# Spreading dense products over the steps of attention, and two more products with the identity

## The chip, the cores and the metric

The kernel runs on one core of a Trainium2 chip. The metric is device time in microseconds (us) of one execution. The time before is 813.35 us, the median of three runs (808.65 to 816.64). PE is the matmul engine, DVE the vector engine, ACT the scalar engine, POOL the general one, SP the engine that issues most DMAs.

## The reference, cut to what matters

Everything is float32. Three blocks follow each other.

```python
def _attn_ref(q_l, k_l, v_l, q_g, k_g, v_g):        # 4 batches, 8 heads, 512 local + 32 global tokens, 64 deep
    out_g = np.matmul(sm(scale * q_g @ k_all.T), v_all)        # the global queries see all 544 keys
    s_ll  = np.where(np.abs(pos[:, None] - pos[None, :]) <= 32, scale * q_l @ k_l.T, -1e9)
    a_l   = sm(concat([scale * q_l @ k_g.T, s_ll]))            # the local ones a band and the 32 global keys
    return concat([out_g, a_l @ concat([v_g, v_l])])
def _moe_ref(x, w_in, w_out, alpha):                 # 2176 tokens, 512 -> 2048 -> 512
    h = x @ w_in
    return (np.maximum(h, 0) + alpha * np.minimum(h, 0)) @ w_out
def _moe2_ref(x, w_gate, w1, w2):                    # 8 experts, 512 -> 1024 -> 512
    ...                                              # greedy assignment of tokens with a capacity per expert
    out[mask] = np.maximum(x[mask] @ w1[e], 0) @ w2[e]
```

`sm` is a softmax over the last axis.

## The kernel before, in words

**Attention** is a loop of 34 steps (`attention`, L491 to L537). A unit is two heads of one batch, a pair is two units, and a pair takes four steps, j = 0 to 3, one for each 128 local queries. The loop is a software pipeline three deep. In step n it makes the scores of step n (PE L388, DVE L394, ACT L396), transposes the probabilities of step n - 1 (PE L410, ACT copy L412, after the DVE normalised them in L404), and multiplies those of step n - 2 with V (PE L421, ACT copy L423).

The work of the global queries of a pair comes in four pieces, one for each step (`pieces`): their scores (L437) at j = 1, nothing at j = 2, their transposes (L461, copied out by ACT and DVE in L462) at j = 3, and their product with V (`gpv`, L471) at j = 0 of the next pair, that is in steps 4, 8, 12, ... 32. L471 is 24 small float32 products of 32 columns.

**Dense work inside attention.** From step BEG = 12 on, PE also does part of the next block for the first 272 tokens (`dense`, L539 to L607). A dense piece is six products of 128x128 by 128x272 (L583, later L591). Two pieces make the first-layer result of one of eight feature blocks f; then comes an epilogue, one step later: ACT L546 (`neg`), DVE L561 (`g`), ACT and POOL L72/L73 (`ghi`, `glo`). The pieces of a step are issued after the scores and ahead of the global piece and of P V. `dense.at` counts them: 20 by the end of step 31, 22 in all.

**Products with the identity.** Before step 12 there is no dense work; there two products of the identity with itself (L521) go into the tile `o`, which P V overwrites afterwards. Nothing reads them.

**Weights.** `fill` puts the decoding of first-layer weights (`win`, eight parts, then `wout`) between the attention's instructions on DVE and ACT: about 2.7 DVE operations of 128x512 in each step. POOL makes the low halves (L73).

**Order.** In attention the orders of PE, DVE and ACT are as written, and a waiting instruction holds up all behind it on its engine. SP and POOL are ordered by the scheduler. After attention only PE keeps the written order; DVE and ACT are scheduled too. There `dense.rest` finishes the first 272 tokens: four results are copied out (ACT L604, `xd`) and stored. The next chunk's products (L200) start in the buffer from which the first of these copies reads. Behind that, PE works through the dense blocks to the end of the program.

Of the kernel before, what the change touches and what calls it, by code (L numbers as in the profile page):

```python
# [25 lines left out]
def tile_attention_moe_moe(ctx: ExitStack, tc: tile.TileContext, qkw, vw,  # L26
# [5 lines left out]
    E, _, FF = w1.shape  # L32
# [279 lines left out]
    with ExitStack() as at:  # L312
# [12 lines left out]
        BEG = SOLO + 4  # L325

        def bank(shape, name):
            pool, tag = pY, "y"
            if name == "s" and wide[0]:
                pool, tag = pS, "s"  # L330
            elif name == "s":
                pool, tag = ((pS, "s"), (pS, "s"), (pH, "h1"), (pH, "h1"))[turn[0] % 4]
                turn[0] += 1
            elif name in ("t", "gs0", "gt0"):
                pool, tag = pX, "x"
            return pool.tile(shape, F32, name=name, tag=tag)

        units = [(b, hp) for b in range(B) for hp in range(H // 2)]
        NU = len(units)
# [4 lines left out]
        STEPS = S // QS  # L344
# [26 lines left out]
        def scores(p, j):  # L371
            d = G[p]
            if j == 0:
                b, hp = units[2 * p]
                if hp == 0:
                    XB[b] = gx.tile([128, KD, ST], F32, name="xb", bufs=2)
                d["x"] = XB[b][:, hp:hp + 2]
            d["pr", j] = pp.tile([128, 4, KW], F32, name="pr")
            d["sm", j] = pp.tile([128, 4], F32, name="sm")
            d["mx", j] = pp.tile([128, 4], F32, name="mx")  # L380
            s = [bank([128, 2, KW], "s") for _ in range(2)]
            for ii in range(0, 4, 2):
                for e in range(2):
                    i = 4 * j + ii + e
                    for a in range(2):
                        u = 2 * p + a
                        for h, r in heads():
                            T.matmul(s[e][lane(2 * a + h, i), ii // 2], queries(u, i)[r], U[u]["k"][r, kpos(i):kpos(i) + KW],  # L388
                                     start=True, stop=True)
            for ii in range(4):  # L390
                i = 4 * j + ii
                m = mask[:, 0 if i == 0 else 2 if i == NQ - 1 else 1]
                sc = pp.tile([128, KW], F32, name="sc", bufs=4)
                V.tensor_tensor_reduce(out=sc, in0=s[ii % 2][:, ii // 2], in1=m, scale=-D ** -0.5, scalar=BIG,  # L394
                                       op0=OP.add, op1=OP.min, accum_out=d["mx", j][:, ii:ii + 1])
                A.activation(out=d["pr", j][:, ii], in_=sc, func=AF.Exp, bias=d["mx", j][:, ii:ii + 1], scale=-1.0,  # L396
                             accum_out=d["sm", j][:, ii:ii + 1])
            P.tensor_scalar(d["sm", j], d["sm", j], 1e-9, None, op0=OP.add)

        def norm(p, j):  # L400
            sm = G[p]["sm", j]
            V.reciprocal(sm, sm)
            pr = G[p]["pr", j]
            V.tensor_tensor(pr, pr, sm.unsqueeze(2).to_broadcast([128, 4, KW]), op=OP.mult)  # L404

        def ptrans(p, j):
            d = G[p]
            t = bank([128, 4, 128], "t")
            for ii in range(4):
                T.transpose(t[:, ii], d["pr", j][:, ii], ident)  # L410
            d["t", j] = tp.tile([128, 4, 128], F32, name="pt")
            A.copy(d["t", j], t)  # L412

        def pv(p, j, o=None):
            d = G[p]
            o = bank([128, 2, QS], "o") if o is None else o
            for ii in range(4):
                i = 4 * j + ii
                for a in range(2):
                    for h, c in heads():  # L420
                        T.matmul(o[c, a, WIN * ii:WIN * ii + WIN], U[2 * p + a]["v"][:, i, c],  # L421
                                 d["t", j][:, ii, lane(2 * a + h, i)], start=True, stop=True)
            at_out[0] = A.copy(d["x"][:, :, SG + QS * j:SG + QS * j + QS], o)  # L423
# [51 lines left out]
        def gout(p):  # L475
            for a in range(2):
                b, hp = units[2 * p + a]
                nc.sync.dma_start(out=xs[hp, :, b * ST:(b + 1) * ST], in_=G[p]["x"][:, a])
                U[2 * p + a] = None
            G[p] = None  # L480
            done[0] = 2 * p + 1
# [9 lines left out]
        def attention():  # L491
            todo = []

            def one():
                if todo:
                    x, f = todo.pop(0)
                    f()
                    yield x

            N = STEPS * NU // 2  # L500
            for n in range(N + 2):
                p, j = divmod(n, STEPS)
                if n < N and p and 2 * p + 2 < NU:
                    (load_qk, load_v)[j // 2](2 * p + 2 + j % 2)
                if n == SOLO - 1:
                    nc.sync.dma_start(out=ag, in_=gate)
                wide[0] = n >= SOLO
                dense.turn(n)
                if 1 <= n <= N:
                    norm(*divmod(n - 1, STEPS))  # L510
                if n < N:
                    scores(p, j)
                while later:
                    later.pop()()
                dense.close(n)
                fill("V", 2)
                o = None
                if n >= 2:
                    o = bank([128, 2, QS], "o")
                    for _ in range((0, 0, 2, 2)[j] if n < BEG else 0):  # L520
                        T.matmul(o[:, 0], ident, ident, start=True, stop=True)  # L521
                dense.products(n)
                for x in one():
                    pass
                fill("V", 2 if n >= SOLO and n % 3 == 0 else 1 if n < SOLO else 0)
                if n >= 2:
                    v, j2 = divmod(n - 2, STEPS)
                    pv(v, j2, o)
                    if j2 == STEPS - 1:
                        gout(v)  # L530
                if 1 <= n <= N:
                    ptrans(*divmod(n - 1, STEPS))
                if n > 2:
                    fill("A", 2)
                if n < N and j == 0:
                    todo += pieces(p)
                yield 0  # L537

        class dense:  # L539
# [24 lines left out]
            def products(n):  # L564
                if n < BEG:
                    return
                for _ in range((0, 1, 2, 1)[n % STEPS] if n < STEPS * NU // 2 else 2):
                    at, dense.at = dense.at, dense.at + 1
                    if at >= 2 * KH + KH - 2:
                        return  # L570
                    if at >= 2 * KH:
                        f, d = divmod(at - 2 * KH, 2)
                        if not f:
                            dense.ys.append(pH.tile([128, CH], F32, name="h1", tag="h1"))
                        for _ in dense.second(d, (2 * f, 2 * f + 1)):
                            pass
                        continue
                    f, half = divmod(at, 2)
                    if not half:
                        dense.ps = pH.tile([128, CH], F32, name="h1", tag="h1")  # L580
                    for k in range(2 * half, 2 * half + 2):
                        for i, (w, x) in enumerate(((0, 0), (0, 1), (1, 0))):
                            T.matmul(dense.ps, WI[0][:, w, k, f * 128:(f + 1) * 128], dense.x[x][:, k],  # L583
                                     start=k == 0 and i == 0, stop=k == KD - 1 and i == 2)
                    if half:
                        dense.over.append((f, dense.ps))
# [22 lines left out]
        def fill(kind, n):  # L609
            if not queue:  # L610
                return
            st, at = queue[0]
            while n and at == kind:
                try:
                    at = next(st)
                    n -= 1
                except StopIteration:
                    queue.pop(0)
                    if ahead_:
                        queue.append(ahead_.pop(0))  # L620
                        queue[-1][1] = next(queue[-1][0])
                    if not queue:
                        return
                    st, at = queue[0]
            queue[0][1] = at
# [48 lines left out]
    with tc.tile_pool(name="dc2", bufs=1, side="right") as dc, tc.tile_pool(name="pW", bufs=2, space=PSUM) as pW, \  # L674
# [4 lines left out]
        n = 0  # L679
# [20 lines left out]
    with ExitStack() as mo:  # L700
# [713 lines left out]
        for k in range(E):  # L1414
            n = 0.0
# [101 lines left out]
```

## Time and profile before

| | |
|---|---|
| median of three runs | 813.35 us (808.65 to 816.64) |
| the profiled execution's own time | 815.25 us |
| its span | 813.5 us |
| PE busy | 784.1 us (96%) |
| DVE busy | 451.3 us (55%) |
| ACT busy | 393.0 us (48%) |
| POOL busy | 371.2 us (46%) |
| mean granted clock of PE | 0.984 of full speed |

The profiled execution lies 1.9 us above the median. Attention ends near 156 us. "Issue" is idle time for which the profile names no releaser. A clock of 1.00 is 2.4 GHz, one of 0.50 is 1.2 GHz.

### The profile page before, as it was taken

The numbers are of one execution on the slowest core, as the hardware profiler recorded it, in microseconds if no ns is written. First come the engines' busy times: TensorE is split into PE (matmuls) and PEld (weight loads), VectorE is DVE, ScalarE is ACT, GpSimd is POOL, SyncE is SP. The second block draws the span as 40 slices with busy tenths as digits, with TensorE's granted clock in tenths as the row PEclk, the third lists the DMA queues.
The fourth block names the chain that finished last, engine by engine and source line by source line (L and its number), as shares of the span: only waits on it lengthen the run. The fifth ranks groups of instructions, "written<-read, shape, count | busy, mean of one in ns | idle before, by whom it ended". The sixth has DMA issues, their size and how long they took to land.

```text
span 813.5 us, 20853 instructions
## 1 busy us (share of the span) xinstructions
PE 784.1 (96%) x8282; PEld 730.3 (90%) x8282; DVE 451.3 (55%) x1547; ACT 393.0 (48%) x983; POOL 371.2 (46%) x348
## 2 busy tenths in 40 slices
PE   7889999999999999999999999999999999999996
PEld 4667777899999999999999999999989999989994
DVE  5888897355546622333343357776767778651210
ACT  5778786554455543333333434342465554454431
POOL 2233343043445443200000647663799989688611
PEclk9989898999999999999999999999999999999999
DMA  9978784343343122021312227333366766457510
GB/s 345 405 253 302 285 290 154 101 168 112 129 134 106 34 78 84 22 62 56 111 56 56 83 67 233 98 106 130 105 212 203 207 206 189 150 186 209 192 52 27
DMA packets 53850, 121.98 MB, mean 150 GB/s; under 512 B 4600, under 2 KB 26040, under 8 KB 51705
## 3 DMA queue, kind: packets, MB, share of 16 engines
q1 hardware_dynamic: 50825, 111.73, 41.8%
q0 software_dynamic: 2928, 8.92, 3.0%
q8 instruction: 65, 1.06, 0.5%
q14 instruction: 32, 0.26, 0.1%
HBM read 102.80 MB, written 17.83 MB: 148 GB/s over the span
## 4 chain that ended last, share of the span: by engine, by line
PE 80%; DVE 6%; issue 4%; ACT 4%; DMA 3%; POOL 2%; POOLq 0%; SPq 0%; DVEq 0%; ACTq 0%
PE h L200 22%; PE h L1273 10%; PE h L1117 10%; PE h L1137 9%; PE y L239 9%; PE o L421 3%; PE s L388 2%; PE t L410 2%; PE go L471 2%; PE h L1350 2%; PE lp L282 2%; ACT pr L396 1%; PE pc L953 1%; DMA raw<-in_moe_w_dram 1%; DMA raw<-in_moe_w_in_dram 1%
## 5 line engine op out<-in xcount | busy, mean ns | idle before, releaser
L73 POOL TENSOR_TENSOR m<-raw,m 128x1024 fp32r<-128x1024 f32 x64 | 152.1, 2400 | 16.4 <-ACT m L72 14.0
L200 PE MATMUL h<-xh,win 128*128 128x272 f32 x704 | 138.3, 291 | 1.5 <-ACT xd L245 1.5
L73 POOL TENSOR_TENSOR gr<-gb,gr 128x272 fp32r<-128x272 f32 x64 | 48.1, 775 | 149.6 <-ACT gr L72 149.2
L200 PEld LDWEIGHTS h<-xh,win 128*128 128x128 f32 x704 | 111.8, 188 | 3.9 <-issue 2.2
L1117 PE MATMUL h<-xsh,m 128*128 128x272 f32 x512 | 103.4, 294 | 0.2 <-issue 0.2
L200 PE MATMUL h<-xl,win 128*128 128x272 f32 x352 | 101.3, 288 | 0.0
L1273 PE MATMUL h<-gr,wout 128*128 128x272 f32 x672 | 95.1, 294 | 0.0
L1137 PE MATMUL h<-hh,m 128*128 128x272 f32 x448 | 91.4, 295 | 0.0
L1273 PEld LDWEIGHTS h<-gr,wout 128*128 128x128 f32 x672 | 87.0, 189 | 0.4 <-ACT gr L72 0.4
L239 PE MATMUL y<-ghi,wout 128*128 128x272 f32 x448 | 86.9, 290 | 0.0
L73 POOL TENSOR_TENSOR glo<-g,ghi 128x272 fp32r<-128x272 f32 x64 | 55.5, 872 | 67.9 <-ACT ghi L72 48.0
L72 ACT CAST m<-raw 128x1024 fp32r<-128x1024 f32 x64 | 65.9, 1049 | 41.6 <-DMA raw<-in_moe_w_dram 40.2
L1117 PEld LDWEIGHTS h<-xsh,m 128*128 128x128 f32 x512 | 81.7, 189 | 0.4 <-DVE home L968 0.4
L205 ACT ACTIVATE neg<-h 128x272 f32<-128x272 f32 x120 | 47.6, 397 | 70.0 <-PE h L200 69.4
L1117 PE MATMUL h<-xsl,m 128*128 128x272 f32 x256 | 74.0, 292 | 0.0
L206 DVE SCALAR_TENSOR_TENSOR g<-neg,al,h 128x272 f32<-128x272 f32 x56 | 27.4, 495 | 83.2 <-ACT neg L205 70.7
L1137 PEld LDWEIGHTS h<-hh,m 128*128 128x128 f32 x448 | 71.4, 188 | 0.9 <-issue 0.9
L239 PEld LDWEIGHTS y<-ghi,wout 128*128 128x128 f32 x448 | 70.9, 188 | 0.8 <-issue 0.8
L200 PEld LDWEIGHTS h<-xl,win 128*128 128x128 f32 x352 | 66.4, 189 | 0.0
L1137 PE MATMUL h<-hl,m 128*128 128x272 f32 x224 | 65.8, 294 | 0.0
L239 PE MATMUL y<-glo,wout 128*128 128x272 f32 x224 | 64.6, 288 | 1.1 <-POOL glo L73 1.1
L206 DVE SCALAR_TENSOR_TENSOR gb<-neg,al,h 128x272 f32<-128x272 f32 x64 | 31.3, 496 | 58.5 <-ACT neg L205 58.4
(286 smaller groups left out, 1650.4 us busy)
## 6 DMA issues: line engine op xcount, KB each, us to landing
raw<-in_moe_w_dram SPq DMA_DIRECT2D x64, 512.0 KB, 4.2
vv<-in_v_dram SPq DMA_DIRECT2D x16, 1024.0 KB
qk<-in_qk_dram SPq DMA_DIRECT2D x14, 720.0 KB, 9.8
raw<-in_moe_w_in_dram SPq DMA_DIRECT2D x16, 512.0 KB, 5.3
raw<-in_moe_w_out_dram SPq DMA_DIRECT2D x16, 512.0 KB, 3.6
xb<-xs SPq DMA_DIRECT2D x15, 544.0 KB, 4.3
xs<-xb SPq DMA_DIRECT2D x16, 272.0 KB, 5.4
xpart<-xd SPq DMA_DIRECT2D x32, 136.0 KB, 1.7
```

Source lines behind the costliest of these rows:

```text
L72: a = A.copy(hi, src)
L73: return a, (lo_eng or V).tensor_tensor(lo, src, hi.bitcast(F32), op=OP.subtract)
L200: T.matmul(ps, wi[:, w, k, fs], x[:, k], start=i == 0, stop=i == 3 * KD - 1)
L205: A.activation(out=neg, in_=ps, func=AF.Relu, scale=-1.0)
L206: epi[0] = V.scalar_tensor_tensor(g, neg, al1[:, hf * KH + f:hf * KH + f + 1], ps, op0=OP.mult, op1=OP.add)
L239: T.matmul(ps, wo[:, w, f, ds_], x[:, f], start=f == 0 and i == 0, stop=f == KH - 1 and i == 2)
L282: T.matmul(lp[r:r + 32], w, x, start=n < 4, stop=n >= LT - 4)
L388: T.matmul(s[e][lane(2 * a + h, i), ii // 2], queries(u, i)[r], U[u]["k"][r, kpos(i):kpos(i) + KW], start=True, stop=True)
L421: T.matmul(o[c, a, WIN * ii:WIN * ii + WIN], U[2 * p + a]["v"][:, i, c], d["t", j][:, ii, lane(2 * a + h, i)], start=True, stop=True)
L1117: T.matmul(ps, d["w1"][:, w, kk, f * 128:(f + 1) * 128], x[:, kk], start=kk == 0 and i == 0, stop=kk == KD - 1 and i == 2)
L1137: T.matmul(ps, d["w2"][:, w, f, ms], x[:, f], start=i == 0, stop=i == 3 * K3 - 1)
L1273: T.matmul(ps[j], wo[:, w, f, ds_], x, start=f == 0 and a == 0, stop=f == KH - 1 and a == 2)
```

## The change

Two lists of numbers are replaced. Products with the identity now also stand at j = 0, which adds two in step 4 and two in step 8, ahead of L471. The dense pieces of steps 12 to 31 go from 0, 1, 2, 1 in the four steps of a pair to 1, 1, 1, 1: one piece is taken from each j = 2 and put in the j = 0 two steps earlier. The number of pieces is unchanged, and by the end of step 31 there are 20 as before.

```diff
                 if n >= 2:
                     o = bank([128, 2, QS], "o")
-                    for _ in range((0, 0, 2, 2)[j] if n < BEG else 0):
+                    for _ in range((2, 0, 2, 2)[j] if n < BEG else 0):
                         T.matmul(o[:, 0], ident, ident, start=True, stop=True)
                 dense.products(n)
...
             def products(n):
                 if n < BEG:
                     return
-                for _ in range((0, 1, 2, 1)[n % STEPS] if n < STEPS * NU // 2 else 2):
+                for _ in range(1 if n < STEPS * NU // 2 else 2):
                     at, dense.at = dense.at, dense.at + 1
```

On PE, step 4 (L388 scores, L471 the global P V, L421 the local P V); the same stands in step 8:

```order
 L388 MATMUL s<-qk 32x128 x16
+L521 MATMUL o<-ident 128x128 x2
 L471 MATMUL go<-gt,vv 64x32 x24
 L421 MATMUL o<-pt,vv 64x32 x16
 L410 MATMUL t<-ident,pr 128x128 x4
```

The two products stand between the scores and the global P V.

On PE, step 12, the first with dense work (`h` is the result of feature block 0):

```order
 L388 MATMUL s<-qk 32x128 x16
+L583 MATMUL h_1122<-xh,win 128x272
+L583 MATMUL h_1122<-xl,win 128x272
+L583 MATMUL h_1122<-xh,win 128x272 x2
+L583 MATMUL h_1122<-xl,win 128x272
+L583 MATMUL h_1122<-xh,win 128x272
 L471 MATMUL go<-gt,vv 64x32 x24
 L421 MATMUL o<-pt,vv 64x32 x16
```

The piece that stood in step 13 is now ahead of the global P V; steps 16, 20, 24 and 28 get theirs in the same place, and one piece goes from each of steps 14, 18, 22, 26 and 30. With that, one of the two epilogues in each pair moves on ACT and DVE from j = 3 to j = 2.

On ACT, just after attention (`xd` are the copies of `dense.rest`, `mag` and `win` the decoding of the second half's weights). Before:

```order
L72 CAST xh<-xb 128x1088
L83 ACTIVATE mag<-raw 128x512
L604 COPY xd<-h_2692 128x272
L83 ACTIVATE mag<-raw 128x512
L604 COPY xd<-h_2781 128x272
L72 CAST win<-mag 128x512
L83 ACTIVATE mag<-raw 128x512
L205 ACTIVATE neg<-h_3099 128x272
```

With the change:

```order
L72 CAST xh<-xb 128x1088
L83 ACTIVATE mag<-raw 128x512 x2
L72 CAST win<-mag 128x512
L604 COPY xd<-h_2607 128x272
L604 COPY xd<-h_2703 128x272
L83 ACTIVATE mag<-raw 128x512
L205 ACTIVATE neg<-h_3103 128x272
```

The first copy now stands behind the second load's first decoding operation and behind the cast of the first part, where before it stood ahead of both.

## Rows read from the trace of the kernel before

**Rows 1.** The page: granted clock in 40 slices, then the chain by engine.

```profile
PEclk9989898999999999999999999999999999999999
...
PE 80%; DVE 6%; issue 4%; ACT 4%; DMA 3%; POOL 2%; POOLq 0%; SPq 0%; DVEq 0%; ACTq 0%
```

**Rows 2.** Stretches (from:to, length, busy by engine, clock, DMA): low clock.

```profile
40.08:43.49 3.41, 3.41 (x56) 2.27 (x54) 0.83 (x6) 1.11 (x3) 0.00 (x0) 0.50 0.41 161
57.15:63.97 6.82, 6.82 (x85) 5.25 (x85) 5.50 (x20) 4.81 (x19) 2.32 (x3) 0.50 0.91 362
94.69:101.52 6.83, 6.83 (x84) 5.15 (x82) 5.30 (x18) 5.09 (x20) 2.76 (x4) 0.50 0.69 250
132.24:139.07 6.83, 6.83 (x101) 5.86 (x102) 3.58 (x17) 2.83 (x12) 1.09 (x2) 0.50 0.30 86
```

**Rows 3.** PE by time (start, length, what, idle before): steps 8, 12, 20, 28.

```profile
37.56 1.94 PE L471 MATMUL go<-gt,vv 128*64 128x32 f32 x46 [0.90 <-issue]
...
54.91 1.59 PE L471 MATMUL go<-gt,vv 128*64 128x32 f32 x39 [0.62 <-ACT gt L462]
56.98 0.75 PE L471 MATMUL go<-gt,vv 128*64 128x32 f32 x9 [0.49 <-issue]
...
93.07 2.07 PE L471 MATMUL go<-gt,vv 128*64 128x32 f32 x48 [1.43 <-ACT gt L462]
...
131.08 0.41 PE L388 MATMUL s<-qk 64*32 64x128 f32 x5 [1.97 <-issue]
131.43 2.61 PE L471 MATMUL go<-gt,vv 128*64 128x32 f32 x48
```

**Rows 4.** PE by time: the global P V of step 16; waits of steps 6 and 10.

```profile
74.67 1.95 PE L471 MATMUL go<-gt,vv 128*64 128x32 f32 x48
...
31.17 0.54 PE L421 MATMUL o<-pt,vv 128*64 128x32 f32 x11 [1.66 <-issue]
...
48.03 1.12 PE L421 MATMUL o<-pt,vv 128*64 128x32 f32 x32 [0.90 <-ACT pt L412]
```

**Rows 5.** Stretches: steps 12 to 27; pairs at full clock; steps 28 to 31.

```profile
55.53:131.43 75.90, 71.38 (x1419) 57.40 (x1415) 67.39 (x251) 61.47 (x213) 30.73 (x40) 0.91 0.83 298
...
74.67:93.07 18.40, 16.73 (x360) 13.65 (x359) 17.40 (x64) 15.22 (x54) 7.79 (x11) 1.00 0.88 328
...
112.13:131.43 19.30, 16.94 (x361) 13.50 (x359) 17.91 (x66) 17.40 (x58) 10.28 (x12) 1.00 0.83 296
131.43:151.28 19.85, 19.85 (x340) 16.81 (x338) 13.14 (x52) 12.11 (x45) 4.03 (x8) 0.83 0.18 59
```

**Rows 6.** PE by time: one pair with the identity, one dense piece, what follows each.

```profile
32.82 0.71 PE L521 MATMUL o<-ident 128*128 128x128 f32 x4
33.37 0.82 PE L461 MATMUL gt<-ident,gpat 128*128 128x128 f32 x6
...
70.76 0.39 PE L583 MATMUL h<-xh,win 128*128 128x272 f32 x1
...
71.62 0.82 PE L461 MATMUL gt<-ident,gpat 128*128 128x128 f32 x6
```

**Rows 7.** ACT by time, step 19: a dense epilogue's cast, and the copy behind it.

```profile
92.14 0.40 ACT L72 CAST ghi<-g 128x272 fp32r<-128x272 f32 x1
92.45 0.57 ACT L462 COPY gt<-gt 128x512 f32<-128x512 f32 x1
```

**Rows 8.** POOL by time: low halves of tokens and weights used by early pieces.

```profile
51.25 1.84 POOL L73 TENSOR_TENSOR xl<-xb,xh 128x544 fp32r<-128x544 f32 x1 [0.31 <-ACT xh L72]
...
56.20 1.35 POOL L73 TENSOR_TENSOR win<-mag,win 128x512 fp32r<-128x512 f32 x1 [0.33 <-ACT win L72]
```

**Rows 9.** After attention: ACT by time, then PE's first product of L200.

```profile
162.25 0.39 ACT L604 COPY xd<-h 128x272 f32<-128x272 f32 x1
...
164.09 0.68 ACT L83 ACTIVATE mag<-raw 128x512 f32<-128x512 f32 x1 [1.46 <-DMA raw<-in_moe_w_in_dram]
...
164.94 0.63 ACT L72 CAST win<-mag 128x512 fp32r<-128x512 f32 x1
...
164.29 0.29 PE L200 MATMUL h<-xh,win 128*128 128x272 f32 x1
```

## The prediction

> **What bounds the kernel now.** I began with the page. PE is in 80% of the chain that ended last, and its granted clock is full everywhere except in the first fifth of the span, in four short dents [rows 1]. So a microsecond that PE loses in attention mostly moves the end, and the dents are the thing to look at. The stretches at low clock, cut out by the clock column, are one of 3.41 us and three of 6.8 us, 23.9 us in all at 1.2 GHz, and PE is busy through all of them [rows 2]. Then I looked at what PE did just before each dent. Each time it was the global P V (L471) of a step with j = 0, namely steps 8, 12, 20 and 28, and each time PE had stood idle beside it: 0.90 us, 0.62 and 0.49 us, 1.43 us, 1.97 us [rows 3]. Two of these five waits are for ACT's copy of the transposed global probabilities (L462); the other three are "issue", with no releaser. The global P V of step 16 came with no wait before it, and no dent followed [rows 4]; the same holds for steps 4, 24 and 32. On the other side, a wait of 1.66 us in step 6 and one of 0.90 us in step 10, in steps with the identity and without L471, were followed by no dent either [rows 4]. So in this trace neither the thin global P V alone nor a wait alone is followed by a fall; the two together are.
>
> Last, what limits attention if PE's clock stays up. In steps 12 to 27 DVE is busy 67.39 of 75.90 us. The pair whose stretch is wholly at full clock from 74.67 to 93.07 took 18.40 us with DVE busy 17.40; the one from 112.13 took 19.30 with DVE busy 17.91. In steps 28 to 31, which decode few weights, DVE has 13.14 of 19.85 us and ACT 12.11 [rows 5]. So DVE is close behind PE until step 27, and far behind it afterwards.
>
> **The change, part by part**, against the profiled execution's 815.25 us.
>
> *Two products with the identity in steps 4 and 8.* A pair of them takes from 32.82 to 33.37 [rows 6], 0.55 us. PE does not wait for anything around L471 of step 4, so there it is a plain cost, and I count it in step 8 too: +1.1. If the "issue" wait of step 8 covers its pair, half of that goes; nothing makes it negative by itself.
>
> *Clock in step 8.* The pair adds full-width products directly ahead of the thin ones. That is what steps 6 and 10 have, which waited and kept the clock. I take it that the 3.41 us come back to full speed: half of it, -1.7. Ends: 0 and -1.7.
>
> *One dense piece ahead of L471 in steps 12, 16, 20, 24 and 28.* A piece takes from 70.76 to 71.62, 0.86 us [rows 6]. It is the same piece that leaves j = 2, so its own time cancels. What is new is that it stands where PE waited for L462: 0.62 us in step 12 and 1.43 us in step 20 [rows 3]. Also, the epilogue that used to end in j = 3 now ends in j = 2, and with it the 0.40 us cast goes that stood directly ahead of L462 on ACT [rows 7]. So the waits for ACT shrink to little, and wide products come before the thin ones. I expect no fall of the clock in steps 12 and 20. In step 28 the 1.97 us "issue" wait may come back, but with a piece behind it.
>
> Does the piece have its operands? Piece 0 in step 12, at 54.3 us (54.91 less the wait of 0.62, [rows 3]), needs the low halves of the tokens, which POOL finished at 53.1. Piece 1 in step 13, a quarter of a pair's 18.40 us later, near 58.9 us, needs the fourth weight part, which POOL finished at 57.6 [rows 8]. Over a microsecond is left in each; a miss would cost that much once.
>
> *What the returned clock is worth in steps 12 to 27.* On PE alone, two dents of 6.82 and 6.83 us would give half, 6.8 us. But DVE's order and work stay the same. In the two pairs at full clock the time exceeded DVE's busy time by 1.00 and 1.39 us [rows 5], mean 1.2. Four pairs at DVE's busy time plus 1.2 make 67.39 + 4.8 = 72.2 us, against 75.90: **-3.7**. Ends: 0, if DVE grows slower beside a busier POOL, and -6.8 by PE. I take the value from the pairs at full clock since they are the nearest rows.
>
> *Steps 28 to 31.* Neither DVE nor ACT is near 19.85 us, so half of 6.83 us comes back: **-3.4**. Ends: 0, if the "issue" wait pulls the clock down again, and -3.4.
>
> *Just behind attention.* The order of ACT changes. The copy `xd` of the first dense result was done at 162.6. PE's first product of L200, in that copy's buffer, came at 164.29 without a wait [rows 9]. Now the copy stands behind the second `mag` (164.09, after a wait for its load) and behind the cast `win` (then from about 164.7, as it needs DVE's decoding). The cast and the copy end near 165.6, so PE waits **+1.3** us for the buffer. Ends: 0, if the load lands sooner or the delay is absorbed at PE's next wait, and 1.6 with the cast where it was. Behind the copy are queued the second copy, two stores on SP and the next epilogues; they have further buffers.
>
> SP's other differences are a weight load moved past two loads of V or past stores of `xs`; these land steps ahead of their use, and I cost them at nothing.
>
> Sum: +1.1 - 1.7 - 3.7 - 3.4 + 1.3 = -6.4, so 815.25 - 6.4 = **808.9 us, say 809**. The profiled execution stood 1.9 us above the median shown, so this is 4.4 us below that median, or 0.5%. A measurement of this kernel can tell about 1% (8.1 us) from no change, and the forecast lies within it.
>
> One rule of the Trainium skill speaks against a part of this. "TensorE: Matmul & The Clock Gate", in its part 4 on the transpose, which it describes as a product with the identity, says that such transposes do not count as PE being busy in the way other products do. If that held for the products with the identity added here, step 8 would keep its dent and the sum would be -4.7, or 810.5. The rows of steps 6 and 10 [rows 4] do not decide it, since no thin product stands there.
>
> **The rivals.**
>
> *Waits alone pull the clock down.* Then only the dents of steps 12 and 20 go, whose waits for ACT are filled. The "issue" waits in steps 8 and 28 are touched by nothing here, and their dents stay. +1.1 - 3.7 + 1.3 = -1.3: 814. For it: every dent has a wait beside it. Against it: steps 6 and 10. Chance 0.17. The same page, in its section on oscillation of the clock gate, puts the fall down to waits between bursts of products; the trace agrees only in part, as steps 6 and 10 waited 1.66 and 0.90 us and kept the clock.
>
> *DVE takes back steps 12 to 27.* The clock stays up, but PE then waits for DVE's `pr` and ACT's copies: +1.1 - 1.7 - 0 - 3.4 + 1.3 = -2.7: 812.5. For it: 17.4 to 17.9 us of DVE work in the pairs without a dent. Against it: these pairs still ended within 1.0 to 1.4 us of that. Chance 0.13.
>
> *DVE doesn't bind.* Its order has slack where PE used to be late. Then PE's own ceiling counts: +1.1 - 1.7 - 6.8 - 3.4 = -10.8: 804.5. Chance 0.12.
>
> *Slower: the dents move to j = 2.* Steps 14, 18, 22, 26 and 30 lose their second piece. If a fall now follows a wait in each, five stretches of 6.8 us instead of three cost 2 x 3.4 = +6.8, with the identity and the buffer +9.2: 824. With only as many dents as before it is +2.4: 817.7. It decides at the point where PE waits in j = 2, where it had no wait until now. Against it: nothing thin stands there besides the local P V, and steps 6 and 10 carry even less dense work. Chance 0.08 for both sizes together.
>
> **How the numbers follow.** The forecast has the remaining 0.50. From 803.5 to 815.5 the range takes in the forecast with the ends of its terms, both rivals at 812.5 and 814, and the one at 804.5. Outside are the slower rival (0.08) and the tails of the run-to-run spread, which was 8 us over three runs, about 0.1 more. Faster by over 1% means below 805.2: the rival at 804.5 and a little of the forecast, 0.15. Slower by over 1% means above 821.5: the larger size of the slower rival, 0.05. Within 1%: 0.80.
>
> **What would show it.** The clock in attention: 1.00 over steps 8 to 32, or at most one dent left. PE's row for L471 in steps 12 and 20 with no wait, or a small one, for L462. Steps 12 to 27 near 72 us, steps 28 to 31 near 16.5 us. A wait of about 1.3 us at the first L200, with ACT's `xd` as its releaser. If the dents remain and have an "issue" wait beside them, the first rival is right. If the clock is full and the pairs still take 18.5 to 19 us, DVE is the bound. If dents follow the steps with j = 2, the slower one is right. What would make the number wrong without touching the mechanism: other "issue" waits than before, since no row says where they come from, and a load that reaches ACT later just behind attention.

## The result, and the profile after

The changed kernel takes **814.13 us** (median of 20 runs, 807.89 to 821.02) against 808.83 us for the kernel before in the same session (20 runs, 803.42 to 818.10). The ratio is 1.0054, with a 95% interval of 1.0032 to 1.0076. So it is slower by half a per cent where a gain of half a per cent was forecast. The time itself lies inside the range given, 803.5 to 815.5 us, and on the 814 of the first rival, but only because the kernel before came out at 808.83 us and not at the 815.25 that the sums start from. The profiled execution took 819.53 us, with a span of 817.8 us and a mean granted clock of 0.985.

Two rows of the page first: the granted clock in 40 slices, and the chain that ended last, by engine.

```profile
PEclk9989997999999999999999999999999999999999
...
PE 71%; DVE 8%; DMA 5%; issue 5%; POOL 5%; ACT 4%; SPq 0%; POOLq 0%; ACTq 0%; DVEq 0%
```

PE's share of the chain is 71%, where it was 80%. The clock's row has two low digits in its first fifth, where it had three [rows 1]. By the clock column there are three low stretches up to 200 us, where there were four [rows 2]. Cut out as stretches (from:to, length, busy time of PE, PEld, DVE, ACT and POOL with instruction counts, clock, DMA share, GB/s), they are:

```profile
38.49:48.75 10.26, 10.26 (x136) 7.77 (x138) 5.19 (x21) 4.87 (x20) 1.56 (x3) 0.50 0.48 194
130.65:140.90 10.25, 10.25 (x129) 8.23 (x129) 5.30 (x22) 4.67 (x20) 1.90 (x4) 0.50 0.21 58
168.26:171.67 3.41, 3.41 (x18) 3.41 (x17) 0.50 (x1) 1.36 (x3) 0.77 (x1) 0.50 0.54 199
```

That is 23.92 us at 1.2 GHz, against 23.9 in the four dents of before [rows 2]. The dents of steps 12 and 20 are gone. Those of steps 8 and 28 are there, three times and one and a half times as long, and there is a new one 11 us behind the last P V. PE by time shows what stands beside them (start, length, what, idle time before):

```profile
38.14 0.29 PE L388 MATMUL s<-qk 64*32 64x128 f32 x1 [1.30 <-issue]
38.36 1.08 PE L521 MATMUL o<-ident 128*128 128x128 f32 x4
39.37 3.21 PE L471 MATMUL go<-gt,vv 128*64 128x32 f32 x48
...
58.76 1.95 PE L471 MATMUL go<-gt,vv 128*64 128x32 f32 x48
...
94.49 1.95 PE L471 MATMUL go<-gt,vv 128*64 128x32 f32 x48
...
129.79 0.44 PE L388 MATMUL s<-qk 64*32 64x128 f32 x12 [1.87 <-issue]
130.16 0.39 PE L591 MATMUL h<-ghi,wout 128*128 128x272 f32 x1
...
131.39 3.21 PE L471 MATMUL go<-gt,vv 128*64 128x32 f32 x48
```

The global P V of steps 12 and 20 has no wait for ACT any more, and the 1.95 us it takes there is what step 16 took at full clock [rows 4]; before it was 1.59 and 0.75 with a pause between them, and 2.07 [rows 3]. Beside that of steps 8 and 28 stands an "issue" wait, as before, 1.30 and 1.87 us long. The clock fell at 38.5 and 130.7 us, right behind these waits and before L471 began, at 39.37 and 131.39. So the thin products had no part in these two falls. The identity products had begun at 38.36 and the dense piece at 130.16, so they came too late to show whether they would have kept the clock up.

Six stretches that cover the whole span, cut at the starts of L471 in steps 4, 12 and 28, at the end of the last P V, and at the 5000th matmul from the end; first the kernel before, then after:

```profile
0.00:19.61 19.61, 13.62 (x258) 8.99 (x259) 10.10 (x50) 10.98 (x41) 4.85 (x25) 1.00 0.91 343
19.61:54.91 35.30, 30.65 (x693) 23.71 (x685) 28.73 (x115) 26.50 (x95) 8.91 (x15) 0.95 0.85 317
54.91:131.43 76.52, 72.00 (x1433) 58.02 (x1433) 68.01 (x251) 62.09 (x214) 31.35 (x40) 0.91 0.83 298
131.43:156.73 25.30, 24.57 (x457) 21.04 (x455) 13.37 (x53) 13.06 (x47) 4.03 (x8) 0.87 0.14 47
156.73:215.84 59.11, 57.61 (x454) 57.23 (x455) 29.96 (x47) 27.52 (x62) 22.92 (x23) 1.00 0.49 160
215.84:813.48 597.64, 585.70 (x5002) 561.26 (x5000) 301.17 (x1033) 252.85 (x527) 299.11 (x239) 1.00 0.38 118
```

```profile
0.00:21.22 21.22, 14.91 (x262) 10.01 (x262) 10.90 (x55) 11.96 (x43) 4.84 (x25) 1.00 0.92 350
21.22:58.76 37.54, 35.13 (x696) 27.23 (x695) 28.37 (x110) 25.78 (x95) 9.34 (x15) 0.86 0.78 286
58.76:131.39 72.63, 67.44 (x1433) 54.14 (x1432) 68.81 (x258) 62.07 (x215) 30.52 (x40) 1.00 0.86 311
131.39:157.12 25.73, 25.00 (x450) 21.04 (x449) 12.33 (x47) 12.20 (x45) 3.29 (x7) 0.81 0.14 46
157.12:219.07 61.95, 59.40 (x454) 58.80 (x455) 30.08 (x47) 28.01 (x62) 22.91 (x23) 0.97 0.47 151
219.07:817.76 598.69, 586.04 (x5002) 561.21 (x5000) 301.22 (x1033) 252.58 (x527) 299.05 (x239) 1.00 0.38 118
```

The differences are +1.61, +2.24, -3.89, +0.43, +2.84 and +1.05 us, together +4.28. Only the third came near its forecast. The fifth, called the **tail** below, is the stretch behind attention. ACT and then PE there:

```profile
161.85 0.67 ACT L83 ACTIVATE mag<-raw 128x512 f32<-128x512 f32 x1 [3.31 <-DMA raw<-in_moe_w_in_dram]
165.52 0.66 ACT L83 ACTIVATE mag<-raw 128x512 f32<-128x512 f32 x1 [3.00 <-DMA raw<-in_moe_w_in_dram]
166.08 0.60 ACT L72 CAST win<-mag 128x512 fp32r<-128x512 f32 x1
166.59 0.67 ACT L604 COPY xd<-h 128x272 f32<-128x272 f32 x2
```

```profile
167.03 0.39 PE L200 MATMUL h<-xh,win 128*128 128x272 f32 x1 [2.18 <-ACT xd L604]
```

The second `mag` waits 3.00 us for its load, where it waited 1.46 [rows 9], and `xd` is queued behind it. So PE waits 2.18 us for `xd`, and 1.2 us later the low stretch from 168.26 begins. The wait of 1.50 us that PE had at 193.14 us in the kernel before (for ACT's `xd` of L245) is gone in turn.

### The profile page after: what moved, and what is told of

Read it like the earlier page. It is cut to its first block, busy times and chain, and to the rows that moved or that the text cites. A ratio compares the mean times of both kernels' runs of the same rounds, so it can differ in the third digit from the quotient of the medians.

```text
span 817.8 us, 20869 instructions
## 1 busy us (share of the span) xinstructions
PE 787.9 (96%) x8290; PEld 732.4 (90%) x8290; DVE 451.7 (55%) x1547; ACT 392.6 (48%) x983; POOL 369.9 (45%) x348
## 4 chain that ended last, share of the span: by engine, by line
PE 71%; DVE 8%; DMA 5%; issue 5%; POOL 5%; ACT 4%; SPq 0%; POOLq 0%; ACTq 0%; DVEq 0%
PE h L200 21%; PE h L1273 10%; PE y L239 9%; PE h L1117 8%; PE h L1137 7%; POOL m L73 3%; PE o L421 2%; DMA raw<-in_moe_w_dram 2%; DMA raw<-in_moe_w_in_dram 2%; PE h L1350 2%; PE lp L282 1%; PE s L388 1%; DVE pr L404 1%; PE go L471 1%; PE t L410 1%
## 5 line engine op out<-in xcount | busy, mean ns | idle before, releaser
L200 PE MATMUL h<-xh,win 128*128 128x272 f32 x704 | 139.8, 293 | 2.5 <-ACT xd L604 2.2
L200 PEld LDWEIGHTS h<-xh,win 128*128 128x128 f32 x704 | 113.0, 190 | 5.1 <-ACT xd L604 2.4
L200 PE MATMUL h<-xl,win 128*128 128x272 f32 x352 | 102.0, 290 | 0.0
L73 POOL TENSOR_TENSOR glo<-g,ghi 128x272 fp32r<-128x272 f32 x64 | 55.1, 866 | 69.7 <-ACT ghi L72 57.6
L200 PEld LDWEIGHTS h<-xl,win 128*128 128x128 f32 x352 | 67.1, 191 | 0.0
```

The source lines that it names most:

```text
L73: return a, (lo_eng or V).tensor_tensor(lo, src, hi.bitcast(F32), op=OP.subtract)
L200: T.matmul(ps, wi[:, w, k, fs], x[:, k], start=i == 0, stop=i == 3 * KD - 1)
```

## The experiments

Each was timed in five rounds beside the kernel before, with 12 runs of its own; one per cent of the time is 8.1 us, and a ratio's interval is about 0.3% either way. "Clock" is the mean granted clock over a kernel's runs; over the 163 runs of the kernel before it is 0.989. A low stretch is one at 1.2 GHz, as a dent is.

**The copy or the work in attention?** In e1, and in all labels with xd_first, the first `xd` is put ahead of the decode on ACT. e2 and e3 have the pieces alone, e4 the identity products alone:

```diff
     def win_part(pool, hf, i):
-        whole(win_steps(pool, hf, i))
+        ...                                    # part 0 up to its Abs, part 1 up to its load
+        with tc.issue_after(dense.freed.ins):  # freed: the copy of the first xd
+            whole(st)                          # the rest of the two
```

e1_after_xd_first: 

> The change, with ACT's copy of the first dense result behind attention put back ahead of the weight decoding, as it stood before. Theory A (the copy's new place is the loss): the 2.2 us wait at the first L200 and the dent behind it go, about 3.2 us, so that the time is at 1.000 to 1.002 of before, with only the 1.1 us of the four identity products left. Rival B (the new work in attention is the loss: the identity, the pieces, the dents of steps 8 and 28): 1.004 to 1.006, as the change itself.

Measured: 813.67 us, ratio 1.0049 (1.0013 to 1.0084), clock 0.991.

e2_pieces_xd_first: 

> One piece in each step, no added identity, the copy ahead of the decoding. Theory A: 0.997 to 1.001, the 1.1 us of the identity less than the first kernel of this set. Rival B with the pieces at fault: 1.004 or more; with the identity at fault: 1.000.

Measured: 812.68 us, 1.0032 (1.0001 to 1.0062), clock 0.991.

e3_pieces_only: 

> One piece in each step, no added identity; here the copy stands behind the decoding as in the change. Theory A: 3 to 4 us (0.4 to 0.5%) slower than the same kernel with the copy first, so 1.002 to 1.005 of before, and a wait of about 2 us at the first L200. Rival B: the same time as that kernel, whatever the wait.

Measured: 813.94 us, 1.0069 (1.0029 to 1.0108), clock 0.990.

e4_identity_xd_first: 

> The identity products in steps 4 and 8 alone, dense pieces as before, the copy ahead of the decoding. Theory A: 1.1 us slower than before, 1.001. Rival B with the identity at fault: 1.003 or more. If the identity keeps the clock up in step 8: 0.998.

Measured: 816.0 us, 1.0073 (1.0041 to 1.0105), clock 0.987.

The place of one copy is not the loss by itself: e1 stays at 1.005. Each half of the change alone also comes out slower here, at 1.003 to 1.007, and the intervals don't tell it from the whole. In e1 the wait at 167 us is gone, but another has taken its place further on. ACT of e1, then PE (line numbers are 7 higher):

```profile
190.75 0.77 ACT L252 COPY xd<-y 128x272 f32<-128x272 f32 x2 [2.20 <-DMA xpart<-xd]
```

```profile
191.18 0.39 PE L207 MATMUL h<-xh,win 128*128 128x272 f32 x1 [2.75 <-ACT xd L252]
```

The third of four `xd` copies waits for the store of the first, since `xd` has two buffers, and PE waits for the copy. In the kernel before the same PE wait was 1.50 us. So in e1 ACT is late again at the end of this stretch, and part of what its beginning gave back is lost there: the tail takes 60.51 us, 61.95 in the changed kernel and 59.11 before.

**The tail's order put back, and taken to the kernel before.** e5, e6 and e7 (change, pieces alone, identity alone) order ACT as Abs (`mag`), `xd`, Abs, `xd`, cast (`win`), and put the first store ahead of the fourth weight load. e8 leaves attention as before and gives the tail the order of the changed kernel; to get it, the first two weight parts are decoded earlier.

e5_after_tail_as_before: 

> The changed kernel with the order just behind attention put back nearly as it was before the change: ACT goes Abs, xd, Abs, xd, win cast (in the first try, e1, the second xd copy still stood behind the win cast and a second Abs), and SP issues the first store of xd ahead of the fourth raw load. In the traces so far the third xd copy waits for the first store (1.13 us before the change, 1.91 in e1, counted on ACT), the Relus behind it on ACT run 1.05 us later against the end of the last P V, and so does the decode that ends in the 2.75 us wait of the first product of the next block for ACT's xd (1.5 before). Theory T (the tail behind attention is worth 2 to 3 of the 5 us): 810.5 to 811.5, ratio 1.002 to 1.0035, what is left being the identity products (1.1 us) and some 1 us of the moved pieces. Rival R (the new work inside attention is the whole loss, whatever stands behind it): ratio 1.005 to 1.006 as in e1.

Measured: 814.28 us, 1.0034 (1.0003 to 1.0065), clock 0.990.

e6_pieces_tail_as_before: 

> Only the pieces (one in each step), no identity products at j = 0, with the order behind attention as before the change. Theory T: ratio 1.000 to 1.002 (in the stretches without low clock the moved pieces cost 0.15 to 0.4 us in each group of four steps, some 1 us in all). Rival R: 1.003 to 1.005, as e2 and e3.

Measured: 814.09 us, 1.0031 (0.9994 to 1.0068), clock 0.990.

e7_identity_tail_as_before: 

> Only the two identity products in each of steps 4 and 8, with the order behind attention as before the change. Theory T: 1.001 to 1.002 (their own 1.1 us), if the mean granted clock is that of the kernel before. Rival R: 1.004 to 1.007 as e4. If the granted clock is again lower than before (0.987 against 0.990 in e4), then the identity products themselves bring low stretches, some 0.75 us per us of lost clock, whatever the tail.

Measured: 814.25 us, 1.0013 (0.9974 to 1.0053), clock 0.989.

e8_before_tail_as_after: 

> The kernel before, attention untouched, with the order just behind attention as the changed kernel has it: ACT goes Abs, Abs, win cast, xd, xd, and SP issues the fourth raw load ahead of the first store of xd. Theory T: 1.0025 to 1.004 (2 to 3 us later; a wait of some 2 us of PE for ACT's xd and, behind it, a possible low stretch). Rival R: 0.999 to 1.001.

Measured: 812.69 us, 1.0017 (0.998 to 1.0053), clock 0.988.

Inconclusive as ratios, and the traces say why. The tail of e5 is no shorter than that of the changed kernel, and that of e8 is shorter than before (e5, then e8):

```profile
151.08:212.78 61.70, 59.17 (x455) 58.77 (x455) 30.09 (x47) 27.90 (x62) 22.93 (x23) 0.97 0.46 149
```

```profile
153.18:211.71 58.53, 57.43 (x455) 57.21 (x455) 28.40 (x47) 27.88 (x63) 22.53 (x23) 1.00 0.50 162
```

Neither kernel had the tail that its name promises. e5 still had PE wait 2.53 us for the third `xd`; e8's earlier decode took that wait away.

**The place in the instruction stream.** In the ten traces so far every "issue" wait of PE above 0.25 us in attention had come at the same count of instructions in PE's stream (matmuls, weight loads and semaphore instructions together): 194 or 195 over a multiple of 256. In the kernels with moved pieces the waits of 1.7 us or more had low stretches beside them. PE of e3:

```profile
95.58 0.53 PE L421 MATMUL o<-pt,vv 128*64 128x32 f32 x5 [2.01 <-issue]
...
118.34 0.83 PE L388 MATMUL s<-qk 64*32 64x128 f32 x21 [2.55 <-issue]
```

Small products ahead of the first scores move all that follows in the stream:

```diff
             N = STEPS * NU // 2
+            o = bank([128, 2, QS], "o")
+            for _ in range(16):                 # 32, 48, 32 in e10, e11, e12
+                T.matmul(o[:1, 0, :1], ident[:, :1], ident[:, :1], start=True, stop=True)
             for n in range(N + 2):
```

e9_after_shift64: 

> The changed kernel with 16 products of one column put ahead of the first scores, where TensorE waits for the first load anyway; nothing else changes but the place of every later TensorE instruction in the instruction stream, some 64 further. In all ten traces so far TensorE's waits that the profile calls issue fall at the same count of TensorE instructions (matmuls and weight loads), 194 or 195 over a multiple of 256. In the kernels with the moved pieces two of them are long (2.0 to 2.3 us some 4.9 us behind the sixth global P V's predecessor, in step 21, and 1.7 to 2.6 us in step 25) and each has a low stretch behind it. Theory F (the loss is where these waits fall): they come at the same counts, so some 2.5 us earlier in the program; lengths change, and the ratio is no longer 1.005: anywhere from 0.998 to 1.006, and at least one of the three shifts (64, 128, 192) gives 1.002 or less. Rival W (the moved work itself costs the time): 1.004 to 1.007 for all three.

Measured: 811.29 us, 1.0021 (0.9988 to 1.0054), clock 0.994.

e10_after_shift128: 

> As e9 with 32 such products, a shift of some 128 instructions, half of a block: the long waits come some 5 us earlier in the program than in the changed kernel. Theory F: another ratio than 1.005, between 0.998 and 1.006, and with e9 and e11 at least one at 1.002 or less. Rival W: 1.004 to 1.007.

Measured: 810.69 us, 1.0017 (0.9983 to 1.005), clock 0.994.

e11_after_shift192: 

> As e9 with 48 such products, a shift of some 192 instructions: the waits come some 7.5 us earlier, or 2.5 us later counted from the block before. Theory F: another ratio than 1.005, and with e9 and e10 at least one at 1.002 or less. Rival W: 1.004 to 1.007.

Measured: 814.12 us, 1.005 (1.0019 to 1.0082), clock 0.992.

e12_before_shift128: 

> The kernel before with 32 products of one column ahead of the first scores: its attention is unchanged, only its instruction stream is shifted by half a block (the order on ACT behind attention comes out as in the changed kernel, which e8 priced at 0.5 us). Theory F: the waits of 0.3 to 2.0 us in its steps 7, 9, 13 and 28 move to other places, so that the time moves too, by as much as 4 us (0.996 to 1.006), and the places of its low stretches with it. Rival W: 0.999 to 1.002, low stretches beside the global P V of steps 12, 20 and 28 as before.

Measured: 815.52 us, 1.0064 (1.0036 to 1.0092), clock 0.985.

The waits moved as the count says. In e9 one stands inside the global P V of step 16, where the unshifted kernel's trace has none:

```profile
76.91 1.30 PE L471 MATMUL go<-gt,vv 128*64 128x32 f32 x29 [0.74 <-issue]
```

Two of three shifts came below 1.0025, with the highest clocks so far, which favours theory F, though the intervals of e9 and e10 reach to that of the unshifted kernel. No shifted trace has the dent of step 28, but among the kernels with the moved pieces only the changed kernel's own trace has it; e1, e2, e3, e5 and e6 have none there either. e12 does not separate the two theories and lies just outside both ranges: its tail came out in the changed kernel's order and took 63.12 us, 4.0 more than before.

**Both, and the buffer.** e13 is the change with e8's tail, e14 adds the shift by 128, e15 is the pieces alone with such a shift, and e16 is the kernel before with three buffers for `xd`:

```diff
-                    xd = gx.tile([128, CH], F32, name="xd", bufs=2)
+                    xd = gx.tile([128, CH], F32, name="xd", bufs=3)
```

e13_after_tail_ahead: 

> The changed kernel with the stretch behind attention as in e8: the first two parts of the second half's weights are decoded some 4 steps of the generator earlier (at 6 and 7 in place of 10 and 20), so that ACT's decode chain no longer ends later than TensorE's block at 190 us. From the last P V to the 5000th matmul from the end e8 took 58.5 us and the kernel before 59.1, the changed kernel 62.0 and e5, e6 and e7, whose order was put back in part only, 61.3 to 61.7. Theory T (this stretch is some 2.5 of the 5 us that the change costs at equal clock): 58 to 59.5 us there, ratio 1.000 to 1.003. Rival N (the stretch evens out, as e5 seemed to say): ratio 1.004 to 1.006.

Measured: 813.97 us, 1.0041 (1.0011 to 1.007), clock 0.990. The tail is 59.84 us; for the time it is a miss for theory T.

e14_shift128_tail_ahead: 

> The changed kernel with the instruction stream shifted by some 128 instructions (e10) and the stretch behind attention as in e13. Theories F and T together: e10's 1.0017 less some 2.5 us, 0.997 to 1.0005, and a mean granted clock of 0.994 or more. If only F holds: 1.001 to 1.003. If the two gains exclude each other because a wait gained ahead is lost at the rendezvous with ACT at 190 us: 1.001 to 1.002, with that wait longer by as much.

Measured: 812.83 us, 1.0026 (0.9994 to 1.0058), clock 0.993. A miss for both together; "only F" fits.

e15_pieces_shift_tail: 

> Only the pieces, no identity products at j = 0, with 36 products of one column ahead of the first scores, so that the blocks of instructions fall on the same products from step 12 on as in e10; the stretch behind attention as the scheduler gives it. Theory F: e10's 1.0017 less the identity products' 1.1 us (0.0014), so 0.999 to 1.002, low stretches as rare as in e10 (mean clock 0.992 or more). Rival W: 1.003 to 1.005, as e3 and e6.

Measured: 814.68 us, 1.0041 (1.0008 to 1.0073), clock 0.991. A miss for theory F.

e16_before_three_xd: 

> The kernel before with a third buffer for xd, so that the third copy doesn't wait for the first store (1.13 us on ACT at 170 us, 2.00 us at 192.7 us, the latter with the first product of the next block waiting 1.50 us behind it). Theory T: that wait of TensorE falls from 1.5 us to 0.5 us or less, ratio 0.997 to 0.9995. Rival N: no change, 0.999 to 1.001.

Measured: 809.91 us, 1.0005 (0.9974 to 1.0036), clock 0.988. By the ratio that is rival N. The wait of 1.50 us is gone from the trace, and the tail is 1.04 us shorter than before, which is less than the ratio can show:

```profile
149.27:207.34 58.07, 57.42 (x455) 57.20 (x455) 29.79 (x47) 27.61 (x63) 23.02 (x23) 1.00 0.50 163
```

In e13 and e14 PE still waited 2.22 and 1.85 us at the first L200 for `xd`. So no kernel with the change had yet been rid of both waits.

**The tail cured whole.** e17 is the changed kernel with the order of e5 and the third buffer of e16; e18 is e17 with the shift of e9.

e17_after_tail_whole: 

> The changed kernel with both halves of the tail's cure: the order behind attention as before the change (e5) and a third buffer for xd (e16), so that neither the first product waits for ACT's xd at 167 us nor the next block's first product at 190 us. Theory T: 58 to 59 us from the last P V to the 5000th matmul from the end (62.0 in the changed kernel, 61.7 in e5, 58.1 in e16), no low stretch there, and 3 us less than the changed kernel: 1.000 to 1.0025 against the kernel before. Rival N: the stretch gets shorter but the time doesn't, 1.004 to 1.006.

Measured: **810.64 us, 0.9997 (0.9958 to 1.0037)**, clock 0.993.

e18_shift64_tail_whole: 

> As e17 with the instruction stream shifted by some 64 instructions as in e9 (1.0021, the highest mean clock of all variants, 0.994, though each trace of it had a low stretch behind attention). Theories F and T together: 3 us less than e9, 0.9975 to 0.9995, mean clock 0.995 or more. Rival N: 1.001 to 1.003.

Measured: **807.89 us, 0.9967 (0.9937 to 0.9997)**, clock 0.996.

The tail of e17, then PE's longest wait for `xd` in it:

```profile
150.48:210.34 59.86, 57.98 (x454) 57.32 (x455) 29.88 (x47) 27.57 (x63) 22.99 (x23) 1.00 0.49 156
```

```profile
188.02 0.39 PE L215 MATMUL h<-xh,win 128*128 128x272 f32 x1 [0.58 <-ACT xd L260]
```

Theory T expected 58 to 59 us there; it is 59.86, 2.1 us less than in the changed kernel, and without a low stretch. In e18's trace (mean clock 0.998) no stretch of attention is at 1.2 GHz any more. The page's row of the granted clock has no low slice, and steps 12 to 27 are at full clock:

```profile
PEclk9999999999999999999999999999999999999999
...
56.38:125.95 69.57, 66.48 (x1433) 53.65 (x1432) 65.42 (x244) 58.69 (x207) 27.92 (x38) 1.00 0.87 312
```

The tail in all 20 traces, us, with PE's longest wait in it for ACT's `xd` (or for another engine, where that is longer), and whether a low stretch lies in it:

```
before 59.11 1.50 no    e5 61.70 2.53 yes   e10 62.01 2.31 yes   e15 62.10 2.36 yes
after  61.95 2.18 yes   e6 61.38 2.31 yes   e11 61.32 1.88 yes   e16 58.07 0.65 no
e1     60.51 2.75 no    e7 61.27 2.19 yes   e12 63.12 2.54 yes   e17 59.86 1.07 no
e2     61.93 2.81 yes   e8 58.53 1.10 no    e13 59.84 2.22 no    e18 59.89 1.06 no
e3     60.42 1.33 no    e9 62.32 2.10 yes   e14 61.70 1.85 yes
e4     61.50 2.25 yes
```

## Why the prediction was wrong

**The step that failed most is the clock that was to come back: -1.7, -3.7 and -3.4, together -8.8 us.** The mean granted clock is 0.9907 over the changed kernel's 20 runs and 0.9888 over the 163 of the kernel before. A straight line through the 399 runs of all kernels, with one slope and one base for each, gives 690 us for a unit of clock. That is an estimate, and by it some 1.3 us came back, so 7.5 of the 8.8 did not. Three things stand in their place, each taken up below: the profiled execution of before had more dents than most, the dents of steps 8 and 28 belong to waits that the change doesn't take away, and a new low stretch came behind attention.

**The second step is "Just behind attention".** It saw the changed order on ACT and the wait for `xd`, priced it at +1.3 with 1.6 as the far end, and stopped at the first product that waits. The wait was 2.18 us, since the load behind which `xd` now stands came later. A low stretch of 3.41 us followed, worth half of that, 1.7; the wait of 1.50 us later on went. Together that is 2.4 of the 2.84 us by which the stretch grew. By the line above, the change costs 4.7 us (+-0.7) at equal clock over the runs, where the prediction's terms without the clock make 2.4 (+1.1 and +1.3).

e17 takes the wait and the low stretch behind attention away, and the ratio falls from 1.0054 to 0.9997. That the tail is part of the loss is shown by this as far as one pair of ratios can (the two intervals just overlap, 1.0032 and 1.0037), but not that it is all of it. The kernel's own median falls by 3.5 us, the rest is the kernel before, which took 808.83 us in one session and 810.63 in the other. By the line, 1.1 us (+-1.1) of it is time at equal clock and 1.5 us is clock (0.9907 to 0.9929). And the third buffer takes away a wait that the kernel before still has: against e16, which has that buffer too, e17 is 4.0 us (+-1.2) slower at equal clock, and level in the median only because its clock is higher (0.993 and 0.988). e18's 0.9967 holds the third buffer and the shift too, so it is no gain of the change alone.

**Some dents went, others stayed or moved.** The forecast was right for steps 12 and 20: their waits for ACT vanished, their dents too, and steps 12 to 27 took 72.63 us where 72.2 was worked out (-3.9 for -3.7, DVE busy 68.81 of it). It was wrong for steps 8 and 28 (-1.7 and -3.4 forecast). As far as these two go, the rival "waits alone pull the clock down" was right: the wait was "issue", and nothing in the change touched it. That its 814 us is what was measured is luck, since it stands for a change of -1.3 us. A wait alone is not always enough either: e18 has one of 1.54 us at 55.54, and no dent. And that rival too took it that the "issue" waits of steps 8 and 28 belong to those steps. They belong to a count of instructions. In e1, e2, e3, e5, e6, e13 and e17 low stretches stand in steps 21 or 25 instead; in e18 there is none. The prediction's last sentence named "issue" waits and a later load behind attention as what could make it wrong, but gave neither a price.

**The base was not typical.** The profiled execution of before had a clock of 0.984, against 0.989 on average. By the line that makes some 3.4 us of the gain that were counted from dents which most runs don't have. I noted the 1.9 us above the median of three runs and did not act on it; the median of 20 runs is 6.4 us lower.

**The identity products.** Forecast +1.1. Up to L471 of step 4, the 7 unshifted traces with them took 20.7 us on average (19.8 to 21.3) and the 6 without 20.0 (19.4 to 20.7), so some 0.7 for the first pair. From there to L471 of step 8, traces without a low stretch and without an "issue" wait above 1 us show no cost (15.7 to 16.4 in six with them, 15.9 to 16.5 in three without). Their purpose was not met: step 8 has a dent in some traces with them (after, e7, e9) and in some without (before, e3). The page "TensorE: Matmul & The Clock Gate" of the Trainium skill, part 4 on the transpose, says that transposes, which it describes as products with the identity, do not count as busy in the way others do. No run here shows whether that holds for plain products with the identity: in step 8 of the changed kernel they began only 0.1 us before the fall.

**The sum, stretch by stretch.** Forecast and measured difference lie 10.7 us apart in the profiled pair (-6.4 and +4.28). From the start to step 12 it is -0.6 against +3.85, so 4.5; in steps 12 to 27 it is -0.2; from step 28 to the last P V -3.4 against +0.43, so 3.8; in the tail +1.3 against +2.84, so 1.5; behind it 1.0. Here too the dents weigh most. Over the runs 7.5 us of clock and 2.3 us of other costs make a miss of 9.8.

**The other rivals.** In the changed kernel's trace steps 12 to 27 ended near DVE's work, as in the forecast, so "DVE takes back" falls. "DVE doesn't bind" stays open: cut as here, PE's ceiling is 76.52 less 6.83, 69.7 us, and e18 took 69.57, but with DVE busy 65.42, so that DVE's work plus 1.2 a pair, 70.2, is as near. That rival's sum also leaves out the +1.3 behind attention without a reason; with it, it is -9.5, or 805.7. "The dents move to j = 2" named the right kind of thing and the wrong place: steps 21 and 25 are j = 1, and their waits are "issue".

**What stays open.** At equal granted clock, by the line above, e17 and e18 are still 3.6 and 3.1 us (each +-0.9) behind the kernel before; they draw level or ahead by having less low clock. About 1.8 of it is found: the identity at the start (0.7), the tail (59.9 against 59.1), and 0.3 from L471 of step 12 to that of step 16, 17.2 us with the pieces moved and 16.9 in e4 and e7. e13 has e17's tail in its trace and not its time (1.0041); its clock, 0.990 against 0.993, suggests that the 2.22 us wait it kept brings a low stretch in other executions, but no trace of it shows that. Why an "issue" wait at one block is 0.3 us and at another 2.5 was not tried on its own; the last section has what the traces show of it.

## What to carry to other kernels

A change early in a program moves, through the scheduler and the instruction stream, things that it does not name; compare all engines' orders for the stretch behind it, and follow a late engine until it has slack again, not just to the first wait. A cure that also helps the kernel before (here the third buffer) has to be put into both before the two are compared. A low stretch of the clock in one trace is a sample: before its return is counted as a gain, look at the mean clock over the runs, and at whether the wait ahead of it belongs to the code or to a place in the instruction stream.

## What the runs showed of the hardware

**PE waits at every 256th instruction, if at all.** All 82 "issue" waits above 0.25 us between 16 and 160 us in 20 traces come at a count of 194 or 195 over a multiple of 256, counted with weight loads and semaphore instructions; they are 0.27 to 2.55 us long. The page's row of the instruction queue goes with it, in the kernel before:

```profile
q8 instruction: 65, 1.06, 0.5%
```

65 packets for 16,692 PE instructions (8,282 matmuls, as many weight loads, 128 others) are 257 for each, near enough to 256; e11 alone, with 16,898, has 66. The packets' times in the traces settle what the waits are for. Each of the 82 ends 0.8 to 1.6 us (median 1.4) after a packet of this queue has landed, and it is always the packet with the number of the block that begins there; at the 351 other block ends of that stretch PE went on a median of 2.6 us behind its packet. So PE waits there for its instructions. The packets come late where loads run: where the DMA engines were less than 30% busy in the 3 us behind a block's end, the packet for the next began a median of 0.3 us after it, and 3.5 us where they were more than 90% busy. No run varied the loads alone. The Trainium skill, "Runtime: NRT & Kernel Launch", section on instruction fetch, states refills in blocks of 256 instructions whose cost is "mostly hidden". The count agrees. The cost was not hidden here: the changed kernel's trace has 1.30 and 1.87 us beside its two longest dents, with the DMA engines 94% and 59% busy in the 3 us up to the end of the wait.

**Waits of some 2 us between dense products mostly had low stretches behind them.** In the tail, where full-width products stand on both sides, 12 of the 14 traces with a wait of 1.85 us or more have a low stretch that begins within 1.3 us of its end (e1 and e13 have none), and none of the 6 with 1.5 or less. So the thin products of L471, which the prediction took as half of the cause, are not needed.
